# Two-stage attention with a cosine-gated feed-forward: the order of ACT's work where batch 0's h ends and batch 1's second softmax begins

## Chip, cores and metric

One core of a Trainium2 chip runs the kernel. The metric is the device time of one execution in microseconds (us); the median of three runs of the kernel before is 249.68 us (249.47 to 250.37). A difference of about 0.5% (1.25 us) is what a measurement can tell from no change.

## The reference

For each of 8 batches and 8 heads, with S = 576 positions, head dimension 64 and 32 packed queries p:

```python
p_packed = sm_attn(p, k, v)               # 32 packed rows a head
out = sm_attn(q, p_packed, p_packed)      # 576 rows a head
x = out.transpose(0, 2, 1, 3).reshape(B * S, H * D)    # 4608 x 512
h = x @ w_in                              # w_in 512 x 2048
g = h * cos(h)
return g @ w_out                          # w_out 2048 x 512, float32 out
```

`sm_attn(q, k, v)` is softmax(q kT / 8) v. All inputs are float32; the kernel loads them as bf16.

## The kernel before

The batches go through a pipeline. For batch b the steps are: `s1` (scores of p with k, exp with a running sum), `a1_pe` (transposes of these weights), `pp` (the packed values: 48 small matmuls into one psum bank, then two copies into `pp_sb`), `pp_T` (two transposes, one copy into `ppT`), `ppw` (the packed values times w_in, in four parts of 512 columns, into `PPW`), `pe_T("q", b)` (24 transposes of q in three groups of eight, each group copied out of psum into `qT`), `s2` (scores of q with the packed keys, two exps), `sums2` (row sums by a matmul with ones, then Ln), `normalise`, and then h: in 16 steps of 128 columns, two or four matmuls of `PPW` with the normalised weights, a cosine on ACT (`Sin` with a bias of pi/2) and a product on DVE that gives `gT`. Last, `out_gen` multiplies `gT` by w_out, 16 matmuls for each chunk of 128 rows. Its matmuls are the filler: `fill(n)` issues the next n of them, `set_filler` starts a new batch's, and `slot` spreads those that are left over the 16 steps of h of the next batch (`keep` of them stay for after it).

The order of each engine's work is the order in which the program issues it (a manual schedule); engines wait for one another by semaphores. Psum has eight banks. Two are output banks (pool `O`, `bank()`), taken in turn. The other six are, by `banks(3)`, three pairs `psA`, or by `banks(0)` six single banks `psH` (`one()`), taken in turn too. A tile in a bank that was used before waits for its last readers. There are three buffers for cosines, so the cosine of a step waits for the product three steps back.

The change lies in the start-up, where batch 0's h is made in single banks by `h_one` (lines 274 to 284), with batch 1 beside it (lines 437 to 470). The steps that matter, in the order issued before: the 16 steps of `h_one(0, fc)`; `pp(1)` after step 13, in an output bank; two warm matmuls (on zeros, for nothing but TensorE's activity, line 376); `pp_T(1)`; two warm matmuls; the load of ACT's table for exp (line 449); the three groups of q1's transposes, copied by ACT, DVE and DVE (line 450); four warm matmuls; issues of loads on POOL's queue; `banks(3)`; `set_filler(0)`; `s2(1)`; `ppw(1, 0)`; one filler matmul; the sums. q of batch 1 (q1) comes by a load that POOL issued much earlier (line 416).

A table load on ACT stands where the program puts it (`preload_act_table_set`). The cosines need the one set, exp and Ln the other; copies run under both.

Of the kernel before, what the change touches and what calls it, by code (L numbers as in the profile page):

```python
# [9 lines left out]
BF16 = mybir.dt.bfloat16  # L10
AF = mybir.ActivationFunctionType
ALU = mybir.AluOpType
PI_HALF = 1.5707963267948966

@with_exitstack
def kernel(
# [15 lines left out]
    NFC = DF // 128  # L32
# [14 lines left out]
    cos_pool = ctx.enter_context(tc.tile_pool(name="cos", bufs=3))  # L47
# [15 lines left out]
    V, ACT, G = nc.vector, nc.scalar, nc.gpsimd  # L63
# [19 lines left out]
    def copy(eng, out, in_):  # L83
        if eng is ACT:
            ACT.copy(out=out, in_=in_)  # L85
        else:
            eng.tensor_copy(out=out, in_=in_)  # L87

    def psa(dt=FP32):
        return psum["A"].tile([128, 2, 512 if dt == FP32 else 1024], dt, name="psA", tag="A")  # L90

    def load(n, b):
        bf[n, b] = bf_pool.tile([TP, H, C * D], BF16, name=n + "bf", tag=n + "bf", bufs=1 if n == "q" else 2)
        G.dma_start(out=bf[n, b], in_=srcs[n][b].rearrange("h (p c) d -> p h (c d)", c=C))  # L94
# [5 lines left out]
    def one(dt=FP32):  # L100
        return psum["H"].tile([128, 512 if dt == FP32 else 1024], dt, name="psH", tag="H")

    def pe_T(n, b, engs=(V, V, V), groups=(0, 1, 2), own=None):
        if 0 in groups:
            xT[n, b] = att_pool.tile([128, H * 3, TP], BF16, name=n + "T", tag=n + "T", bufs=2 if n == "k" else 1)
        t = xT[n, b]
        flat = bf[n, b].rearrange("p h x -> p (h x)")
        for i in groups:
            ps = own(BF16) if own else psa(BF16)[:, 0, :]
            for j in range(8):  # L110
                o = 8 * i + j
                nc.tensor.transpose(ps[:, j * TP:(j + 1) * TP], flat[:, o * 128:(o + 1) * 128],
                                    ident[0:TP, 0:TP])
            copy(engs[i], t[:, 8 * i:8 * i + 8].rearrange("p a x -> p (a x)"),
                 ps[:, 0:8 * TP])

    def bank(dt=FP32):
        return O.tile([128, 512 if dt == FP32 else 1024], dt, name="ot", tag="ot")
# [33 lines left out]
    def recips(b):  # L152
        r1[b] = small.tile([128, 2], FP32, name="r1")
        rs1[b] = small.tile([128, 2], FP32, name="rs1")
        V.reciprocal(r1[b], sums1[b])
        V.tensor_scalar(out=rs1[b], in0=r1[b], scalar1=scale, scalar2=None, op0=ALU.mult)
# [16 lines left out]
    def pp(b, eng=V, own=None):  # L173

        ps = own() if own else psa()[:, 0, :]
        for y in range(2):
            for j in range(C):
                c = 2 * (j % 3) + j // 3
                for x in range(4):
                    nc.tensor.matmul(ps[32 * x:32 * x + 32, y * D:(y + 1) * D],  # L180
                                     a1T[b][0:TP, y, j, 32 * x:32 * x + 32],
                                     bf["v", b][:, 2 * x + y, c * D:(c + 1) * D],
                                     start=(j == 0), stop=(j == C - 1))
        t = pp_sb[b % 2].rearrange("p a d -> p (a d)")
        copy(eng, t[:, 0:2 * D], ps[:, 0:2 * D])
        copy(eng, t[:, 2 * D:3 * D], ps[:, 0:D])

    def pp_T(b, eng=V, own=None):
        ps = own(BF16) if own else psa(BF16)[:, 0, :]
        t = pp_sb[b % 2].rearrange("p a d -> p (a d)")  # L190
        for i in range(2):
            nc.tensor.transpose(ps[:, i * 128:(i + 1) * 128], t[:, i * D:i * D + 128], ident)
        copy(eng, ppT[b % 2].rearrange("p i x n -> p (i x n)"), ps[:, 0:256])

    def ppw(b, n, eng=None, own=False, later=False, cuts=((0, 512),)):
        if b not in PPW:
            PPW[b] = ppw_pool.tile([128, 2, DF], BF16, name="PPW", tag="PPW")
        two = isinstance(eng, tuple)
        if own:
            ps = [bank(), bank()]  # L200
        else:
            t = psa()
            ps = [t[:, 0, :], t[:, 1, :]]
        for x in range(4):
            for y in range(2):
                r = slice(64 * y, 64 * y + 64)
                nc.tensor.matmul(ps[y][32 * x:32 * x + 32, :], ppT[b % 2][r, 0, x, :],  # L207
                                 w_in_bf[r, x, n * 512:(n + 1) * 512], start=True, stop=True)

        def evacuate(cuts=cuts):  # L210
            if own or two:
                for a, z in cuts:
                    for y in range(2):
                        copy(eng[y] if two else eng, PPW[b][:, y, n * 512 + a:n * 512 + z], ps[y][:, a:z])
            else:
                copy(eng or (V, ACT)[n % 2], PPW[b][:, :, n * 512:(n + 1) * 512], t)
        if later:
            return [lambda c=c: evacuate((c,)) for c in cuts]
        evacuate()
# [8 lines left out]
    def sums2(b, y):  # L228
        if b not in lns:
            lns[b] = att_pool.tile([128, 2, S], FP32, name="lns", tag="lns")  # L230
        ps = psa()
        for e in range(2):
            nc.tensor.matmul(ps[:, e, 0:HS], ones_blk, a2u[b][:, y, e * HS:(e + 1) * HS],  # L233
                             start=True, stop=True)
        ACT.activation(out=lns[b][:, y].rearrange("p (e x) -> p e x", e=2),  # L235
                       in_=ps[:, :, 0:HS], func=AF.Ln)
# [9 lines left out]
    gT, joint = {}, {}  # L246
# [22 lines left out]
    def g_tile(b):  # L269
        gT[b] = g_pool.tile([128, NFC, S], BF16, name="gT", tag="gT")  # L270
        if b % 2 == 0:
            joint[b // 2] = j_pool.tile([128, NFC, 128], BF16, name="joint", tag="joint")

    def h_one(b, fc):

        if fc == 0:
            g_tile(b)
        ps = one()
        for y in range(2):
            nc.tensor.matmul(ps, PPW[b][:, y, fc * 128:(fc + 1) * 128], a2n[b][:, y, 0:512],  # L280
                             start=(y == 0), stop=(y == 1))
        cs = cos_pool.tile([128, 512], BF16, name="cosT")
        ACT.activation(out=cs, in_=ps, func=AF.Sin, bias=PI_HALF)  # L283
        V.tensor_tensor(out=gT[b][:, fc, 0:512], in0=ps, in1=cs, op=ALU.mult)  # L284

    def h_rest(b):

# [67 lines left out]
    def fill(n):  # L355
        while n > 0 and filler[1] > 0:
            next(filler[0])
            filler[1] -= 1
            n -= 1
# [13 lines left out]
    def warm(n, wps=None, w=None):  # L373
        wps, w = bank() if wps is None else wps, wz if w is None else w
        for _ in range(n):
            nc.tensor.matmul(wps, w[:, 0:128], w, start=True, stop=True)  # L376
# [60 lines left out]
    banks(0)  # L437
    a1_pe(1, own=one)
    recips(1)
    for fc in range(NFC):  # L440
        h_one(0, fc)
        if fc in (0, 4, 8):
            ppw(0, 1 + fc // 4, (ACT, ACT if fc == 8 else V), own=True)
        if fc == 13:
            pp(1, ACT, own=bank)
    warm(2)
    pp_T(1, ACT, own=bank)
    warm(2)
    ACT.preload_act_table_set(EXP_SET)  # L449
    pe_T("q", 1, (ACT, V, V), own=one)  # L450
    warm(4)
    load("v", 2)
    load("q", 2)
    load("k", 3)
# [2 lines left out]
    set_filler(0)  # L457
    s2(1)
    ppw(1, 0, V)
    fill(1)  # L460
    sums2(1, 0)
    fill(1)
    sums2(1, 1)
# [28 lines left out]
    def cross(n, b):  # L492
# [43 lines left out]
                                in_=p_bf[:, 8:2 * B].rearrange("p g t d -> p (g t d)"))  # L536
# [73 lines left out]
```

## Time and profile before

| what | value |
|---|---|
| median of three runs | 249.68 us |
| profiled execution: time, and its span | 249.53 us, 247.6 us |
| granted TensorE clock | 1.00 |
| last h_one cosine (L283), last product (L284) start | 32.75 us, 33.73 us |
| exp table's load (L449) | 33.66 to 34.94 us |
| ACT's copy of q1's group 0 (L85) | 34.95 to 35.75 us |
| first exp of s2(1) (L225) | 36.24 us |
| first filler matmul, first sums matmul | 36.39 us, 37.03 us |

The span is the time from the first to the last recorded work; the time is 1.9 us more. Starts are in us from the span's start. PE is TensorE's matmuls, PEld its weight loads, DVE VectorE, ACT ScalarE, POOL GpSimd, SP SyncE; L283 is line 283 of the kernel before. Many copies have the line of a helper (85 on ACT, 87 on DVE), so they are told apart by their tiles: `pp_sb`, `ppT`, `qT`, `PPW`. Matmuls overlap in the rows: one of 512 columns shows 0.38 us, but the next starts 0.216 us after it.

### The profile page before, as it was taken

How to read it: one execution, taken by the hardware profiler on the slowest of the kernel's cores; microseconds unless marked ns; L12 is line 12 of the kernel's file. 1: busy time of each engine (PE TensorE's matmuls, PEld its weight loads, DVE VectorE, ACT ScalarE, POOL GpSimd, SP SyncE). 2: the span in 40 equal slices, each digit the busy share in tenths (PEclk: the TensorE clock that was granted, in tenths of full speed). 3: DMA queues.
4: the chain of work that ended last, by engine and by line, in shares of the span. 5: the costliest groups of instructions: out<-in, count | busy, mean ns of one | idle time of the engine just before them, and what ended most of it. 6: DMA issues, size and time to landing. Idle time of an engine off the chain costs nothing.

```text
span 247.6 us, 5423 instructions
## 1 busy us (share of the span) xinstructions
PE 234.0 (95%) x2204; PEld 128.3 (52%) x2240; DVE 158.5 (64%) x244; ACT 170.3 (69%) x284; POOL 38.2 (15%) x61
## 2 busy tenths in 40 slices
PE   7988889999989999999999999999999999999993
PEld 3453344566445554565446554565456554665452
DVE  3369977676549777578757666578756685774000
ACT  2369998677568777888787677978886685874110
POOL 8532330200400041005000500030000000000000
PEclk9999999999999999999999999999999999999999
DMA  6999999999899999996999894989292113111123
GB/s 88 204 209 209 202 208 228 202 235 176 135 186 173 218 146 201 189 221 122 215 214 197 148 222 109 184 172 203 63 187 59 42 45 84 43 34 53 52 75 85
DMA packets 63992, 37.37 MB, mean 151 GB/s; under 512 B 36592, under 2 KB 59376, under 8 KB 63968
## 3 DMA queue, kind: packets, MB, share of 16 engines
q0 software_dynamic: 23184, 18.81, 50.0%
q1 hardware_dynamic: 40624, 18.09, 35.6%
q8 instruction: 17, 0.28, 0.5%
q10 hardware_dynamic: 160, 0.13, 0.2%
q14 instruction: 7, 0.06, 0.1%
HBM read 37.22 MB, written 9.44 MB: 188 GB/s over the span
## 4 chain that ended last, share of the span: by engine, by line
PE 82%; DMA 6%; DVE 4%; ACT 3%; issue 2%; POOL 2%; DVEq 0%; ACTq 0%; POOLq 0%
PE ot L339 48%; PE psA L254 22%; DMA w_in_bf<-in_moe_w_in_dram 6%; PE psA L207 3%; PE psA L137 2%; PE ot L325 1%; PE psA L233 1%; PE psA L180 1%; DVE gT L284 1%; PE psH L280 1%; DVE PPW L87 1%; ACT a2u L225 1%; DVE gT L261 1%; POOL kbf L94 1%; ACT L449 1%
## 5 line engine op out<-in xcount | busy, mean ns | idle before, releaser
L339 PE MATMUL ot<-w_out_bf,gT 128*128 128x512 bf16 x482 | 128.2, 379 | 2.8 <-issue 1.9
L261 DVE TENSOR_TENSOR gT<-psA,cosT 128x576 bf16<-128x576 f32 x112 | 83.5, 757 | 32.4 <-ACT cosT L258 31.5
L258 ACT ACTIVATE cosT<-psA 128x576 bf16<-128x576 f32 x112 | 73.0, 653 | 26.4 <-PE psA L254 24.8
L254 PE MATMUL psA<-a2n,PPW 128*128 128x288 bf16 x448 | 73.2, 286 | 0.0
L339 PEld LDWEIGHTS <-gT 128*128 128x128 bf16 x512 | 47.3, 98 | 43.5 <-issue 7.8
L254 PEld LDWEIGHTS <-PPW 128*128 128x128 bf16 x448 | 43.8, 98 | 30.5 <-issue 1.0
L87 DVE CAST PPW<-psA 128x1024 bf16<-128x1024 f32 (+1 forms) x25 | 26.1, 1050 | 7.7 <-PE psA L207 6.0
L87 DVE COPY osb<-ot 128x512 f32<-128x512 f32 (+1 forms) x14 | 9.4, 671 | 21.3 <-PE ot L325 17.4
L85 ACT COPY osb<-ot 128x512 f32<-128x512 f32 (+1 forms) x23 | 13.2, 575 | 13.5 <-PE ot L339 12.4
L265 POOL COPY joint<-gT 128x512 bf16<-128x512 bf16 x14 | 8.6, 617 | 88.4 <-DVE gT L261 88.4
L243 DVE SCALAR_TENSOR_TENSOR a2n<-a2u,r,lns 128x576 bf16<-128x576 bf16 x16 | 12.4, 814 | 8.1 <-ACT lns L241 8.1
L146 ACT ACTIVATE a<-psA 128x576 bf16<-128x576 f32 x16 | 10.3, 646 | 8.3 <-PE psA L137 8.3
L235 ACT ACTIVATE lns<-psA 128x576 f32<-128x576 f32 x16 | 10.3, 651 | 6.5 <-PE psA L233 5.9
L339 PE MATMUL ot<-w_out_bf,joint 128*128 128x512 bf16 x47 | 12.6, 379 | 0.1
L376 PE MATMUL ot<-wz 128*128 128x512 bf16 (+1 forms) x23 | 10.2, 548 | 2.0 <-DVE wz L390 1.7
L225 ACT ACTIVATE a2u<-psA,rs 128x576 bf16<-128x576 f32 x16 | 11.0, 738 | 1.5 <-PE psA L137 1.4
L207 PE MATMUL psA<-w_in_bf,ppT 64*32 64x512 bf16 x224 | 10.4, 380 | 0.2
L284 DVE TENSOR_TENSOR gT<-psH,cosT 128x512 bf16<-128x512 f32 x16 | 9.9, 682 | 0.4 <-ACT cosT L283 0.4
L241 ACT ACTIVATE lns<-lns 128x576 f32<-128x576 f32 x16 | 10.0, 674 | 0.0
L85 ACT CAST PPW<-psA 128x1024 bf16<-128x1024 f32 (+1 forms) x9 | 7.4, 825 | 2.8 <-PE psA L207 2.8
L283 ACT ACTIVATE cosT<-psH 128x512 bf16<-128x512 f32 x16 | 8.7, 619 | 0.9 <-issue 0.4
L280 PE MATMUL psH<-a2n,PPW 128*128 128x512 bf16 x30 | 7.9, 381 | 0.9 <-DVE PPW L87 0.6
(90 smaller groups left out, 163.8 us busy)
## 6 DMA issues: line engine op xcount, KB each, us to landing
kbf<-in_k_dram POOLq DMA_DIRECT2D x8, 576.0 KB, 13.5
vbf<-in_v_dram POOLq DMA_DIRECT2D x8, 576.0 KB, 7.4
qbf<-in_q_dram POOLq DMA_DIRECT2D x8, 576.0 KB, 10.6
out_dram<-osb SPq DMA_DIRECT2D x24, 192.0 KB, 2.8
out_dram<-osb SPq DMA_DIRECT2D x22, 128.0 KB, 2.9
w_in_bf<-in_moe_w_in_dram POOLq DMA_DIRECT2D x4, 512.0 KB, 16.6
w_out_bf<-in_moe_w_out_dram POOLq DMA_DIRECT2D x4, 512.0 KB, 21.2
out_dram<-osb SPq DMA_DIRECT2D x26, 64.0 KB, 2.1
```

The lines of the kernel that those rows point to most:

```text
L85: ACT.copy(out=out, in_=in_)
L87: eng.tensor_copy(out=out, in_=in_)
L146: ACT.activation(out=a1[b % 2][:, y, :, 0:TP].rearrange("p (e m) x -> p e m x", e=2), in_=ps[y][:, :, 0:HS].rearrange("p e (m x) -> p e m ...
L207: nc.tensor.matmul(ps[y][32 * x:32 * x + 32, :], ppT[b % 2][r, 0, x, :], w_in_bf[r, x, n * 512:(n + 1) * 512], start=True, stop=True)
L225: ACT.activation(out=a2u[b][:, y].rearrange("p (e x) -> p e x", e=2), in_=ps[y][:, :, 0:HS], func=AF.Exp, scale=rs1[b][:, y:y + 1])
L243: V.scalar_tensor_tensor(out=a2n[b][:, y], in0=a2u[b][:, y], scalar=r1[b][:, y:y + 1], in1=lns[b][:, y], op0=ALU.mult, op1=ALU.mult)
L254: nc.tensor.matmul(ps[:, e, 0:HS], PPW[b][:, y, fc * 128:(fc + 1) * 128], a2n[b][:, y, e * HS:(e + 1) * HS], start=(y == 0), stop=(y == 1))
L258: ACT.activation(out=csv, in_=ps[:, :, 0:HS], func=AF.Sin, bias=PI_HALF)
L261: V.tensor_tensor(out=gT[b][:, fc, :].rearrange("p (e x) -> p e x", e=2), in0=ps[:, :, 0:HS], in1=csv, op=ALU.mult)
L280: nc.tensor.matmul(ps, PPW[b][:, y, fc * 128:(fc + 1) * 128], a2n[b][:, y, 0:512], start=(y == 0), stop=(y == 1))
L284: V.tensor_tensor(out=gT[b][:, fc, 0:512], in0=ps, in1=cs, op=ALU.mult)
L339: nc.tensor.matmul(pss[c], w, w_out_bf[:, fc, :], start=(fc == 0), stop=(fc == NFC - 1))
```

## The change

`h_one` is cut in three: the call issues the matmuls and gives back a function that issues the cosine, and this one gives back a function that issues the product. It also takes the bank to write to. Steps 0 to 12 are issued as before. Of the last three steps the matmuls stay in their order on TensorE, and ACT and DVE get a new order:

- ACT: the two copies of `pp(1)`, cosine 13, the copy of `pp_T(1)`, cosines 14 and 15, the copy of q1's group 0, the exp table's load. Before: cosine 13, the copies of `pp(1)`, cosines 14 and 15, the copy of `pp_T(1)`, the load, the copy of group 0.
- DVE: products 13 and 14, the copies of q1's groups 1 and 2, product 15. Before: products 13 to 15, then the copies.
- Step 15's psum is an output bank, and so the filler's first tile takes that bank.
- Two groups of two warm matmuls and one of four, in output banks, become one of four (after `pp_T`) and one of three (after q1's transposes), in psH banks.
- Ahead of the sums of batch 1 stand two filler matmuls where there was one, and `slot(1)` has one less to spread.

```diff
-    def h_one(b, fc):
+    def h_one(b, fc, own=None):
 
         if fc == 0:
             g_tile(b)
-        ps = one()
+        ps = (own or one)()
         for y in range(2):
             nc.tensor.matmul(ps, PPW[b][:, y, fc * 128:(fc + 1) * 128], a2n[b][:, y, 0:512],
                              start=(y == 0), stop=(y == 1))
-        cs = cos_pool.tile([128, 512], BF16, name="cosT")
-        ACT.activation(out=cs, in_=ps, func=AF.Sin, bias=PI_HALF)
-        V.tensor_tensor(out=gT[b][:, fc, 0:512], in0=ps, in1=cs, op=ALU.mult)
+
+        def cos():
+            cs = cos_pool.tile([128, 512], BF16, name="cosT")
+            ACT.activation(out=cs, in_=ps, func=AF.Sin, bias=PI_HALF)
+            return lambda: V.tensor_tensor(out=gT[b][:, fc, 0:512], in0=ps, in1=cs, op=ALU.mult)
+        return cos
...
-    for fc in range(NFC):
-        h_one(0, fc)
+    for fc in range(13):
+        h_one(0, fc)()()
         if fc in (0, 4, 8):
             ppw(0, 1 + fc // 4, (ACT, ACT if fc == 8 else V), own=True)
-        if fc == 13:
-            pp(1, ACT, own=bank)
-    warm(2)
+    c13 = h_one(0, 13)
+    pp(1, ACT, own=bank)
+    c13()()
+    c14 = h_one(0, 14)
+    c15 = h_one(0, 15, own=bank)
     pp_T(1, ACT, own=bank)
-    warm(2)
+    c14()()
+    rest15 = c15()
+    warm(4, one())
+    pe_T("q", 1, (ACT, V, V), (0,), own=one)
     ACT.preload_act_table_set(EXP_SET)
-    pe_T("q", 1, (ACT, V, V), own=one)
-    warm(4)
+    pe_T("q", 1, (ACT, V, V), (1, 2), own=one)
+    rest15()
+    warm(3, one())
     load("v", 2)
     load("q", 2)
     load("k", 3)
...
     ppw(1, 0, V)
-    fill(1)
+    fill(2)
     sums2(1, 0)
```

## Prediction

> **What bounds the kernel now.** First I read the page's line of engines and the busy time by stretch (columns: length, then busy us and instructions of PE, PEld, DVE, ACT, POOL, then granted clock, DMA share, GB/s).
>
> ```profile
> PE 234.0 (95%) x2204; PEld 128.3 (52%) x2240; DVE 158.5 (64%) x244; ACT 170.3 (69%) x284; POOL 38.2 (15%) x61
> ```
> ```profile
> 28.00:36.20 8.20, 7.31 (x126) 3.73 (x120) 6.94 (x12) 7.69 (x15) 2.19 (x4) 1.00 1.28 205
> 36.20:38.20 2.00, 1.39 (x21) 0.58 (x7) 1.21 (x1) 1.96 (x4) 0.50 (x1) 1.00 1.24 207
> 38.20:63.00 24.80, 24.52 (x206) 14.56 (x209) 17.54 (x26) 18.42 (x29) 2.21 (x3) 1.00 1.25 205
> ```
>
> From 38.2 us PE is the bound: 0.28 us idle of 24.80. Around the change, 28 to 38.2, it is not: there ACT is the full one (1.96 of 2.00 in the second row). So I read the chain of waits there (start, length, what).
>
> ```profile
> 32.75 0.63 ACT cosT L283
> 33.38 0.27 ACT ppT L85
> 33.64 0.02 issue
> 33.66 1.28 ACT L449
> 34.94 0.01 issue
> 34.95 0.81 ACT qT L85
> 35.76 0.04 issue
> 35.80 0.36 PE psA L137 x8
> ...
> 36.24 1.37 ACT a2u L225 x2
> 37.61 0.55 ACT lns L235
> 38.16 0.04 issue
> 38.20 0.41 PE psA L207 x8
> ```
>
> Here the exp table's load (L449) stands ahead of ACT's copy of q1, the scores (L137) wait for that copy, and the first exp (L225, 36.24) for the scores. While PE makes the scores, ACT idles 0.48 us. From the first exp the chain runs on ACT to 38.16 and goes over to PE at 38.20; after that PE hardly waits. So a microsecond gained at the first exp is one gained at the end. Third, PE's own rows, and the load of q1:
>
> ```profile
> 30.41 0.56 PE L180 MATMUL ot<-vbf,a1T 96*32 96x64 bf16 x48
> 32.44 0.27 PE L192 MATMUL ot<-ident,pp_sb 128*128 128x128 bf16 x2
> 33.16 1.20 PE L112 MATMUL psH<-ident,qbf 96*128 96x96 bf16 x24
> 36.39 0.39 PE L339 MATMUL ot<-w_out_bf,gT 128*128 128x512 bf16 x1
> 37.03 0.41 PE L233 MATMUL psA<-a2u,ones_blk 128*128 128x288 bf16 x2 [0.25 <-ACT a2u L225]
> ```
> ```profile
> L94 POOL DMA_DIRECT2D qbf<-in_q_dram x1: 801/801/801, 15.0 to 15.0; - x1
> DMA to landing us min/median/max: 18.2/18.2/18.2
> ```
>
> q1 was issued at 15.0 and landed 18.2 us later, at 33.2; its transposes begin at 33.16. So the copy of group 0 can't begin before about 33.7, whatever ACT's order is: 8 transposes at 0.043 us (24 start within 0.99 us) and the last one's 0.21 end at 33.68.
>
> **ACT, step by step.** No work goes or comes on ACT; its order changes. Starts follow each other by 0.49 us after a cosine, 0.15 and 0.10 after the two pp copies, 0.42 after the ppT copy (all starts in ACT's rows).
> - cos 12 starts at 30.92 as now. The pp product ends at 30.97, so the two pp copies go at 31.41 and 31.56 (now 32.01, 32.16), ahead of cos 13, at 31.66 (now 31.52).
> - The ppT transposes follow the second copy's end (31.79): 31.84 to 32.11. ppT is copied at 32.15 (now 33.23), cos 14 goes at 32.6 (now 32.26), cos 15 at 33.1 (now 32.75). Each cosine also needs the product three steps back on DVE (three cos buffers): those of steps 10, 11, 12 end at 31.42, 32.02, 32.62, so they don't hold them.
> - ACT is free at 33.58 and waits 0.14 for the q1 transposes. Copy of group 0: 33.72 to 34.52 (0.80). Load: 34.53 to 35.82 (1.28). First exp: 35.83, if the scores are there.
> - Gain at the first exp: 36.24 − 35.83 = 0.41 us. It is less than the 0.48 of the gap that closes plus what ACT did earlier, as q1's landing is late next.
>
> **DVE and the scores.** The scores need all three q copies, two of them on DVE. Cos 14 ends 0.33 later (33.22), so its product runs 33.25 to 33.93 (now 33.13 to 33.81). Group 1's copy waits for its transposes (34.02): 34.06 to 34.61, group 2's 34.53 to 35.08. The product of step 15, now ahead of them (33.73 to 34.41), comes after: 35.00 to 35.68. Scores: 35.12 to 35.56, under the load, with 0.26 us to spare. That the last product reads an output bank and no psH bank is what lets the scores' psA banks, cut from the psH ones, open without it.
>
> **The new wait.** The filler's first psum tile takes the output bank of step 15, so its first matmul (L339) waits for that product: 35.68. Behind it on PE stand the second filler matmul and the sums (L233), which ACT's ln and so all else need. PPW's 8 matmuls (0.41) after the scores end at about 35.8, so the wait costs nothing, and two fillers at 0.216 end at 36.2. The sums wait for the first exp's end, 35.83 + 0.74 = 36.57, anyway: 0.4 us of cover. Without it each us of lateness would cost one.
>
> **fill(1) → fill(2).** Now one filler starts at 36.39, the sums at 37.03: 0.42 idle, a second one fits. It is then one less of the 48 dealt out in slot(1) (64 − 12 − 4), where PE is the bound: −0.22. Bounds 0 (it leaves a gap there) and 0.22; I take 0.22, by the 0.28 idle us in 24.80.
>
> **The rest at nothing, and why.** Warm matmuls go from eight to seven; four start behind the ppT transposes at 31.95 and end issuing at 32.8, before q1 lands, three fill 34.19 to 34.84 before the scores. Cover gone, they would cost 0.22 each. The psH tiles they take were freed by products ended at 30.8 and 33.2. DMAs: no load changes place. On POOL the load of q2 still waits for the last q1 transpose (34.36), v2's stands ahead as now; SP's first output write is 13 us away. w_out's four parts land at 35.7, 38.9, 41.2 and 43.8 (issue plus landing); fillers 1, 9, 17 and 25 need them at 36.39, 39.85, 42.56 and 46.20 now, and at most 0.65 earlier after: the closest keeps 0.3. The later PE-bound stages only shift; from 43 us on the list of waits has PE waiting 2.7 us in total, none of it for a DMA.
>
> **Sum.** 0.41 + 0.22 = 0.63 us off the profiled execution: span 247.60 → 246.97, time 249.53 → 248.90. The runs' median is 249.68, 0.15 above that execution; from it, 249.05.
>
> **A rule against this change.** The trace first: both loads around here take 1.28 us; the first begins 0.02 after the copy ahead of it and the copy behind it begins 0.01 after. The Trainium skill, "ScalarE: Activation LUTs", section What ACT_TABLE_LOAD costs, gives the same load about 1283 ns, but adds a drain of about 1380 ns for every switch. By the page, a load placed directly ahead of the exp would delay it by that too, an estimate of 249.05 + 1.38 = 250.43. No row here has such a drain, so the sum goes without.
>
> **Rivals.**
> - **The load loses its cover (slower).** Now a late q1 hides under the load: with landing at L, the first exp comes at max(34.95, L + 0.56) + 1.28; after, at max(33.58, L + 0.56) + 2.11. At L = 33.16 the second wins by 0.41, at 33.57 they tie, from 34.39 on it loses 0.83. For it: 18.2 us in a queue at a DMA share of 1.24 to 1.3, seen once. Against: what is ahead of q1 in the queue isn't touched, and a stream that is late as a whole also delays ACT, whose work here began with w_in's landing at 19.72. Time: 249.68 + 0.83 − 0.22 = 250.29. Chance 0.12.
> - **The scores aren't hidden.** If DVE's products slip by over 0.26 (cos 14 is already 0.33 later) the exp waits for the scores again; slipping 0.66 eats the 0.41. For: DVE is full here (back to back from 30.13 to 35.34). Against: group 1's copy is held by the transposes, not by DVE. Only the filler stays: 249.46. Chance 0.13.
> - **The filler brings nothing**: its step in slot(1) becomes a gap in which cosine or product is awaited: 249.27. Chance 0.10.
> - **More than that**: one filler less moves every deal in slot(1) and the order around it; at most the 0.28 and the 1.71 idle us of PE up to 120 us (55.29 of 57.00 busy from 63) could come back. It needs most of a further 0.6 to pass 248.4. Chance 0.08.
>
> **Numbers.** The forecast has the remaining 0.57. 0.5% is about what a measurement of this kernel can tell from no change, that is 248.43 to 250.93. The forecast and both partial rivals lie within it; the late landing too, unless a run at the upper end (0.69 over the median) comes with it, a third to half of its chance. Faster 0.08, same 0.87, slower 0.05. The range, 248.5 to 250.0, holds the forecast with the runs' own scatter and the partial rivals, and leaves out the late landing and the larger gain.
>
> **What would show it.** In the profile after: pp's copies ahead of cos 13; the load starting where the group-0 copy ends, near 34.5; the exp starting at most 0.05 after the load, near 35.8; no idle time of ACT put down to L137; the step-15 product after both q copies and before the first L339; two L339 matmuls ahead of the first L233; ppw's second part near 37.8. The prediction is wrong if the exp waits for PE, if q1 lands later than 33.6, if an L339 or L233 matmul waits for L284's product, or if the 0.41 is there at 38 us and gone at 63.

## The result, and the profile after

The kernel after takes 249.09 us (median of 16 runs, 248.89 to 249.71), the kernel before, on the same chip, 249.68 us (16 runs, 249.1 to 251.22). The ratio is 0.9973, with a 95% interval of 0.9960 to 0.9985: 0.67 us, and between 0.37 and 1.0. (0.67 is also the difference of the two means, 249.81 and 249.14; the medians lie 0.59 apart.) The forecast was 249.05. But its two terms didn't both hold, as the trace shows.

The profiled execution after took 249.57 us (span 247.8), one of the longest of its kernel, so its total says nothing about the gain; its stages do. First the chain of waits from 33 to 38 us (start, length, what), which answers to the one shown of before:

```profile
33.65 0.77 ACT qT L85
34.42 0.02 issue
34.43 1.08 ACT L457
35.51 0.21 issue
35.73 0.75 ACT a2u L225
36.48 0.04 issue
36.52 0.40 PE psA L233 x2
36.92 0.22 PE ot L342
```

The copy of q1 comes first, the load (L457) behind it, and the first exp starts at 35.73 instead of 36.24. The scores (L137) are gone from the chain. (The chain books the last 0.21 us of the load as "issue"; in its row below the load runs to 35.71.) In ACT's rows of the same kernel the new order can be read, and that ACT waits for nothing any more (no bracket at the row of the exp):

```profile
31.46 0.43 ACT L85 CAST pp_sb<-ot 128x128 bf16<-128x128 f32 x2
31.71 0.69 ACT L285 ACTIVATE cosT<-psH 128x512 bf16<-128x512 f32 x1
32.25 0.41 ACT L85 COPY ppT<-ot 128x256 bf16<-128x256 bf16 x1
...
33.62 0.80 ACT L85 COPY qT<-psH 128x768 bf16<-128x768 bf16 x1
34.43 1.28 ACT L457 ACT_TABLE_LOAD   x1
35.73 1.37 ACT L225 ACTIVATE a2u<-psA,rs 128x576 bf16<-128x576 f32 x2
```

Where do the 0.51 us go? The starts of h's cosines and of the table loads, before and after, worked out from both traces:

```
                                  before    after
first exp of s2(1)                 36.24    35.73   -0.51
first cosine of slot(1)            41.40    40.89   -0.51
exp table's load after slot(1)     62.68    62.28   -0.40
pp of batch 3 (first matmul)       84.26    84.40   +0.14
last table load                   210.16   210.30   +0.14
```

Two things are lost, one after the other: 0.11 in slot(1), and 0.55 just ahead of batch 3's pp. The second one's cause stands in the waits between 78 and 96 us of the kernel after (who waited for whom: us, times, longest):

```profile
PEld L180 <- DMA a1T<-a: 1.1, 1, 1.1
PE psA L180 <- DVE PPW L87: 0.8, 1, 0.8
```

Batch 3's transposed weights, which SP sends through a DMA, landed late, at 84.36 us (before: 82.44). The row of PE's own wait names a cast on DVE. PE's rows at that place, first before, then after:

```profile
84.26 0.55 PE L180 MATMUL psA<-vbf,a1T 96*32 96x64 bf16 x48 [0.27 <-DVE gT L261]
```
```profile
84.40 0.56 PE L180 MATMUL psA<-vbf,a1T 96*32 96x64 bf16 x48 [0.82 <-DVE PPW L87]
```

In the kernel after the cast ended at 84.40, just when pp began. But pp doesn't need it: in the kernel before the same cast ran from 84.13 to 84.81, and pp began at 84.26, behind the product of L261. DVE's rows up to there are those of before, 0.41 earlier, so without the late weights pp would have begun at about 83.85. It is the weight load (PEld) that waits, for the DMA.

### The profile page after: what moved, and what is told of

Read it like the earlier page. It is cut to its first block, busy times and chain, and to the rows that moved or that the text cites. A ratio compares the mean times of both kernels' runs of the same rounds, so it can differ in the third digit from the quotient of the medians.

```text
span 247.8 us, 5456 instructions
## 1 busy us (share of the span) xinstructions
PE 238.0 (96%) x2239; PEld 128.3 (52%) x2239; DVE 158.2 (64%) x244; ACT 170.0 (69%) x284; POOL 38.1 (15%) x61
## 4 chain that ended last, share of the span: by engine, by line
PE 80%; ACT 5%; DVE 4%; issue 1%; DVEq 0%; ACTq 0%
PE ot L342 48%; PE psA L254 21%; PE psA L207 3%; PE psA L137 2%; ACT cosT L285 2%; PE psA L233 2%; DVE gT L286 1%; PE ot L328 1%; PE psA L180 1%; DVE PPW L87 1%; ACT cosT L258 1%; DVE gT L261 1%; ACT a2u L225 1%; DVE joint L300 0%; PE psA L192 0%
## 5 line engine op out<-in xcount | busy, mean ns | idle before, releaser
L342 PE MATMUL ot<-w_out_bf,gT 128*128 128x512 bf16 x512 | 133.2, 380 | 0.0
L261 DVE TENSOR_TENSOR gT<-psA,cosT 128x576 bf16<-128x576 f32 x112 | 83.5, 756 | 33.2 <-ACT cosT L258 32.2
L85 ACT COPY osb<-ot 128x512 f32<-128x512 f32 (+1 forms) x23 | 13.2, 576 | 13.5 <-PE ot L342 12.4
L243 DVE SCALAR_TENSOR_TENSOR a2n<-a2u,r,lns 128x576 bf16<-128x576 bf16 x16 | 12.4, 813 | 8.2 <-ACT lns L241 8.2
L379 PE MATMUL ot<-wz 128*128 128x512 bf16 (+1 forms) x17 | 9.0, 639 | 1.9 <-DVE wz L393 1.7
L286 DVE TENSOR_TENSOR gT<-psH,cosT 128x512 bf16<-128x512 f32 x15 | 9.3, 681 | 0.4 <-ACT cosT L285 0.4
## 6 DMA issues: line engine op xcount, KB each, us to landing
qbf<-in_q_dram POOLq DMA_DIRECT2D x8, 576.0 KB, 11.1
```

What stands on the lines that cost most here:

```text
L243: V.scalar_tensor_tensor(out=a2n[b][:, y], in0=a2u[b][:, y], scalar=r1[b][:, y:y + 1], in1=lns[b][:, y], op0=ALU.mult, op1=ALU.mult)
L261: V.tensor_tensor(out=gT[b][:, fc, :].rearrange("p (e x) -> p e x", e=2), in0=ps[:, :, 0:HS], in1=csv, op=ALU.mult)
L286: return lambda: V.tensor_tensor(out=gT[b][:, fc, 0:512], in0=ps, in1=cs, op=ALU.mult)
L342: nc.tensor.matmul(pss[c], w, w_out_bf[:, fc, :], start=(fc == 0), stop=(fc == NFC - 1))
```

## The experiments

All were run beside the kernel before on the same chip; a ratio is against that kernel. One number serves throughout: how long after the first matmul of batch 1's pp the first exp of `s2(1)` starts. Both stand behind the same earlier work, so it is free of what happened before 30 us, as long as q1's landing doesn't set the exp. It is 5.83 in the kernel before and 5.28 in the execution after shown above, where q1's landing did set it.

**1. The load back ahead of the copy.**

```diff
-    pe_T("q", 1, (ACT, V, V), (0,), own=one)
     ACT.preload_act_table_set(EXP_SET)
+    pe_T("q", 1, (ACT, V, V), (0,), own=one)
     pe_T("q", 1, (ACT, V, V), (1, 2), own=one)
```

> The kernel after, with the exp table's load put back ahead of ACT's copy of q1's group 0; all else as after. Theory (the gain is made where the load hides the scores): ACT is free at 33.55, loads to 34.85, copies to 35.65, the scores follow and the first exp starts near 36.13, 0.40 later than after: about 249.5. Rival 1 (the gain comes from the earlier pp copies, the output bank and the fuller fillers): the exp may move, the time stays near 249.1. Rival 2 (the gain is only a narrower scatter of the landings): 249.1 to 249.7, with the exp's start following q1's landing.

Measured: 249.45 us, ratio 1.0004 [0.9990, 1.0019], no gain left. ACT's rows:

```profile
33.44 1.28 ACT L456 ACT_TABLE_LOAD   x1
34.73 0.80 ACT L85 COPY qT<-psH 128x768 bf16<-128x768 bf16 x1
36.02 1.37 ACT L225 ACTIVATE a2u<-psA,rs 128x576 bf16<-128x576 f32 x2 [0.48 <-PE psA L137]
```

The 0.48 us of idle ahead of the exp is back, and the exp starts 5.79 after pp (before: 5.83). With everything else of the change in place, the earlier pp copies and the output bank are worth 0.04 here. The gain hangs on the order of copy and load; rival 1 falls. Nor is rival 2, a narrower scatter of the landings alone, enough: q1 landed at 33.01 us here and at 33.02 in the kernel after, and the exp came at 36.02 and not at 35.73.

**2. One filler matmul instead of two.**

```diff
     ppw(1, 0, V)
-    fill(2)
+    fill(1)
     sums2(1, 0)
```

> The kernel after, with one filler matmul instead of two ahead of the sums. Theory after reading the trace (the second filler is given back in slot(1), whose cosines and copies set its pace): first exp unchanged near 35.7, slot(1) ends within 0.1 of where it ended after, time 249.0 to 249.15. Rival (the prediction's term): 0.22 slower, 249.3.

Measured: 249.31 us, ratio 0.9981 [0.9962, 1.0000]. The runs lie up to 1.8 us apart (248.70 to 250.52), so the time doesn't decide. The trace does: from the first cosine of slot(1) to the next table load 21.27 us pass, as before (21.28); in the kernel after 21.39. This held in every trace of the study: 21.27 to 21.28 in the seven with one filler ahead of the sums, 21.39 to 21.40 in the seven with two. The second filler is not worth 0.22 us, it costs 0.11. PE's rows from 53 us show one place, first before, then after:

```profile
54.03 0.65 PE L254 MATMUL psA<-a2n,PPW 128*128 128x288 bf16 x4
54.63 0.50 PE L112 MATMUL psA<-ident,kbf 96*128 96x96 bf16 x8
54.97 0.81 PE L339 MATMUL ot<-w_out_bf,gT 128*128 128x512 bf16 x3
```
```profile
53.52 0.65 PE L254 MATMUL psA<-a2n,PPW 128*128 128x288 bf16 x4
54.33 0.50 PE L112 MATMUL psA<-ident,kbf 96*128 96x96 bf16 x8 [0.16 <-ACT kT L85]
54.67 0.81 PE L342 MATMUL ot<-w_out_bf,gT 128*128 128x512 bf16 x3
```

Four matmuls of 288 columns take 0.49 us, so 0.11 us of idle stand behind them before, and 0.32 after: with the deal moved, k2's transposes come before ACT has emptied the bank they need. At 49.3 us it is the same: one filler fewer is dealt ahead of step 6's matmuls (two and not three by the program; of the three of before, only two have a record in the trace), and 0.30 us of idle, waiting for a product on DVE, stand there instead of 0.09. A third gap, 0.11, is gone; in sum the 0.22 saved and 0.11 more are spent waiting.

This trace shows a second thing. PE's waits from 16 to 18.5 us:

```profile
PE ot L112 <- DMA kbf<-in_k_dram: 0.9, 1, 0.9
```

k1's load, unchanged and issued at 5.0 us in all kernels, landed 12.4 us later here and 11.4 later in the trace before; and as k1's transposes stand between the sums of batch 0, pp of batch 1 came at 30.96 instead of 30.41. Of the twelve traces of the study in which k1's load is unmoved, eight have it 11.1 to 11.6 us after its issue, four (experiments 2, 3, 4 and 8) 12.4 to 12.7. With a late k1 pp thus came 0.55 us later and more, which is one cause that the scatter of the runs can have; runs without a trace can't be sorted by it. The first exp stands 5.20 after pp here.

**3. The swap alone, in the kernel before.**

```diff
-    ACT.preload_act_table_set(EXP_SET)
-    pe_T("q", 1, (ACT, V, V), own=one)
+    pe_T("q", 1, (ACT, V, V), (0,), own=one)
+    ACT.preload_act_table_set(EXP_SET)
+    pe_T("q", 1, (ACT, V, V), (1, 2), own=one)
```

> The kernel before, with nothing but ACT's copy of q1's group 0 put ahead of the exp table's load. Theory: ACT copies from 33.7 to 34.5 and loads to 35.82; DVE, in its old order, ends the last q copy at 35.34, so the scores run 35.39 to 35.83 and the exp starts near 35.9: 0.33 to 0.36 earlier than before, about 249.3. Rival (the other parts are needed: the output bank and the product's place keep the scores from being late): the exp stays within 0.15 of 36.24, no difference from before.

Measured: 249.33 us, ratio 0.9987 [0.9969, 1.0006]. In the trace k1 was late (pp at 31.24), and the exp stands 5.42 after pp, 0.41 nearer than before: two lines of the change make 0.41 of the 0.63 that the whole change gives where k1 is late (5.20, experiment 2). Most of what is left is DVE, which in the old order makes product 15 ahead of the q copies (they end at 36.17 here); ACT's exp waits for the scores again (start, length, the bracket is idle time):

```profile
35.20 1.28 ACT L450 ACT_TABLE_LOAD   x1
36.67 1.37 ACT L225 ACTIVATE a2u<-psA,rs 128x576 bf16<-128x576 f32 x2 [0.18 <-PE psA L137]
```

**4. Two fillers alone, in the kernel before** (`fill(1)` to `fill(2)`).

> The kernel before, with nothing but two filler matmuls instead of one ahead of batch 1's sums. Theory (given back in slot(1)): first exp as before, time within 0.1 of before. Rival (the prediction's term): 0.22 faster. A third way: the second filler delays the sums, by 0.0 to 0.1, as there are 0.42 us of idle for its 0.22.

Measured: 250.36 us, ratio 1.0021 [1.0003, 1.0040]. No gain: the runs are, if anything, longer. The exp stands 5.83 after pp, so the sums aren't delayed, and slot(1) takes 21.39. The rival's 0.22 is off by its sign, and the theory's nothing by 0.1.

**5 and 6. q1 landing 2.5 us later**, in the kernel before and after:

```diff
-    load("q", 1)
-    for n in range(4):
+    load_w_out(0)
+    load("q", 1)
+    for n in range(1, 4):
         load_w_out(n)
```

> The kernel before, with the load of q1 issued behind the first part of w_out instead of ahead of it, so that q1 lands about 2.5 us later (near 35.7). Theory (the load hides a late q1): with L the start of q1's transposes, ACT has loaded the table by 34.95 and waits; copy at L + 0.56, first exp at L + 1.84, near 37.5, about 1.3 us later than before: 250.6. A late k1 hardly shows, as L sets the time. Rival (ACT's own order of work sets it): the exp stays within 0.5 of 36.24.

> The kernel after, with the same later load of q1. Theory (the copy ahead of the load takes the load's cover away): copy at L + 0.56, load, first exp at L + 2.67, near 38.4: 0.83 later than in the kernel before with the same late load, 0.9 to 1.0 longer with the second filler's cost: about 251.5. Rival (the change is better whatever q1 does): it keeps 0.3 or more of its lead over the kernel before with the late load.

Measured: 252.99 us, ratio 1.0136 [1.0108, 1.0164], and 252.56 us, ratio 1.0107 [1.0078, 1.0135]. The kernel after was not the longer one, against the theory, and the first exps came at 39.64 and 38.76 instead of 37.5 and 38.4. But the pair can't decide: while PE waited for q1 its clock fell. The busy times by stretch of the first of them (the number behind POOL's is the granted clock):

```profile
33.00:35.60 2.60, 0.22 (x2) 0.03 (x2) 1.47 (x3) 1.98 (x3) 0.00 (x0) 1.00 1.27 204
35.60:39.00 3.40, 3.40 (x28) 2.30 (x28) 1.12 (x2) 0.80 (x1) 1.04 (x2) 0.51 1.25 207
```

2.4 us without a matmul were followed by 3.4 us at half clock, in which the transposes and the four warm matmuls went at half speed, ahead of the scores. In the second, 2.7 us without a matmul were followed by 3.4 us at half clock from 36.43 on, over the three warm matmuls and the scores.

**7 and 8. q1 landing 1.25 us later, with the clock kept up.** The load stands between two halves of w_out's first part, and five more warm matmuls stand ahead of q1's transposes:

```diff
-    load("q", 1)
-    for n in range(4):
+    load_w_out(0, 0, 2)
+    load("q", 1)
+    load_w_out(0, 2, 4)
+    for n in range(1, 4):
         load_w_out(n)
```

> The kernel before, with q1's load issued between two halves of w_out's first part (so that it lands about 1.25 us later, near 34.4) and five more warm matmuls ahead of q1's transposes, which keep TensorE from idling while it waits. Theory (the table's load hides it): first exp at max(34.95, L + 0.56) + 1.28, 36.24 to 36.3 with L near 34.4, as before without the delay; with the same TensorE clock all along, 249.3 to 249.5 when k1 lands early. Rival (any delay of q1 shows): 1.25 later.

> The kernel after, with the same later load and five more warm matmuls. Theory (the copy waits, and the table's load waits behind it): first exp at L + 2.67, near 37.05, 0.8 later than in the kernel before with the same delay, and with the second filler's 0.11 about 0.9 longer. Rival (the change keeps its lead): first exp before 36.2.

Measured: 250.07 us, ratio 1.0012 [0.9996, 1.0028], and 250.64 us, ratio 1.0045 [1.0027, 1.0063]. Now the kernel after is the longer one, by 0.57. With L the start of q1's transposes (34.19 and 34.74; in the second, k1 was late and the nine warm matmuls end only at L), the first exp came at L + 2.43 before and at L + 2.66 after. ACT's rows of the second:

```profile
35.29 0.80 ACT L85 COPY qT<-psH 128x768 bf16<-128x768 bf16 x1 [0.89 <-PE psH L112]
36.10 1.28 ACT L459 ACT_TABLE_LOAD   x1
37.40 1.37 ACT L225 ACTIVATE a2u<-psA,rs 128x576 bf16<-128x576 f32 x2
```

The sum for the kernel after was right (L + 2.67). For the kernel before it wasn't: 36.61 and not 36.3. Its chain says why:

```profile
34.19 1.19 PE psH L112 x24
35.38 0.86 PE ot L376 x4
36.24 0.30 PE psA L137 x8
36.54 0.03 ACTq L225
36.57 0.04 issue
36.61 1.37 ACT a2u L225 x2
```

Behind a late q1 the load is hidden, as claimed, but all 24 transposes, DVE's two copies (they ended at 36.10) and the scores are not. (The chain goes by the four warm matmuls between them on PE instead. The last one began at 35.87, so the scores could follow at 36.08: without the copies too they would have come only 0.1 earlier than at 36.17.) So the price of the lost cover is 2.66 − 2.43 = 0.23 us, and not 0.83. With the second filler's 0.11 that makes 0.34 of the 0.57 in the times; the rest isn't settled (L itself differs by 0.56 in these two executions).

**9 and 10. k1 made late in every execution**, by issuing it between two halves of w_in's first part, before and after:

```diff
-    load("k", 1)
-    for n in range(3):
+    load_w_in(0, 0, 2)
+    load("k", 1)
+    load_w_in(0, 2, 4)
+    for n in range(1, 3):
         load_w_in(n)
```

> The kernel before, with w_in's first part loaded in two halves and k1's load issued between them, so that k1 lands late (near 17.6) in every execution and the rest of the stream stands as it was. Theory (the executions fall in two groups by whether k1 lands near 16.4 or 17.5): the runs form one group, the late one, near 250.3 with pp of batch 1 at 31.1 and the first exp 5.83 after it. Rival (the groups come from something else): two groups again, 249.3 and 250.3.

> The kernel after, with k1 late in the same way. Theory (with everything up to h later, q1 has landed in good time, and ACT's order alone sets the copy, so the earlier pp copies count too): first exp 5.20 after pp of batch 1, 0.63 earlier than in the kernel before with a late k1; less 0.11 for the second filler, 0.5 shorter, near 249.7. Rival (the gain is the same 0.3 in both groups): first exp 5.4 after pp, 0.3 shorter.

Measured: 252.95 us, ratio 1.0134 [1.0101, 1.0166], and 251.90 us, ratio 1.0090 [1.0065, 1.0114]. k1 came later than meant (its transposes at 18.74 and 19.34, with 3.4 us at half clock from 20.4 and 20.5), and the expected times were missed by 2.2 to 2.7 us. The runs of the kernel before with a late k1 still form two groups (252.1 to 252.2 and 253.7 to 254.2), as the rival had it: whether k1's landing still varied or the groups come from something else, one trace of each kernel can't tell. What the pair does settle is the number: 5.83 from pp to the exp before, 5.20 after, 0.63 us. When pp comes late enough for q1 to lie ready, the gain is 0.63 and not 0.41.

**11. After, unchanged, once more.**

> The kernel after, unchanged, beside the others on the same chip. Theory: two groups of executions by k1's landing, 0.3 below those of the kernel before where k1 is early and 0.5 where it is late; first exp 5.20 after pp of batch 1 where q1 has landed in time; slot(1) takes 22.09 again. The 0.56 that the first execution lost at pp of batch 3 comes back only if the transposed weights land after 83.5. Rival (that loss belongs to the change): it is there again.

Measured: 249.17 us, ratio 0.9988 [0.9972, 1.0003]. Exp 5.20 after pp, slot(1) 21.39, and no loss at batch 3's pp: the stages from there on run 0.23 ahead of the trace before, in which pp of batch 1 stood 0.29 earlier: together 0.52. The theory's part on k1 was wrong here: k1 landed 11.3 us after its issue, yet pp came at 30.70, since the first transposes, k0's, came 0.65 later than before (8.27 for 7.62). The interval is wide: it holds no difference as well as the first measurement's 0.9973.

The rows of the late DMA, in this execution (first) and in that of the kernel after that lost 0.55 us:

```profile
L160 SPq DMA_TRANSPOSE a1T<-a x1: 4830/4830/4830, 70.6 to 70.6; - x1
...
DMA to landing us min/median/max: 12.2/12.2/12.2
```
```profile
L160 SPq DMA_TRANSPOSE a1T<-a x1: 4630/4630/4630, 70.5 to 70.5; - x1
...
DMA to landing us min/median/max: 13.9/13.9/13.9
```

Issued at the same time, they landed at 82.8 and 84.4; pp began at 84.03 here and would have begun at about 83.85 there. Landing shortly before them (by 0.2 to 0.5 us, and by 0.2 to 0.8 in all fourteen traces) is the load of k4, the last of three that POOL issues from 66.3 us on in this execution and from 67.75 in the one that lost, when k3's transposed copy has landed. That copy was late in turn behind q2's load, which was issued at 34.6 in both and landed at 55.36 here and at 56.24 there; SP transposes q2 before k3. Both links, from q2's load to k4's and from there to the weights, are argued from these times; neither was tried. So it isn't the change alone. In the kernel before, with pp at 84.26, weights landing at 84.36 would have cost about 0.14; the change uses up the rest of the slack, as PE gets there 0.41 earlier and the landing doesn't.

**12. A version that should beat both**: after with one filler, and q1's groups of 6, 9 and 9.

```diff
+    def pe_T(n, b, engs=(V, V, V), groups=(0, 1, 2), own=None, at=(0, 8, 16, 24)):
...
-    pe_T("q", 1, (ACT, V, V), (0,), own=one)
+    pe_T("q", 1, (ACT, V, V), (0,), own=one, at=(0, 6, 15, 24))
     ACT.preload_act_table_set(EXP_SET)
-    pe_T("q", 1, (ACT, V, V), (1, 2), own=one)
+    pe_T("q", 1, (ACT, V, V), (1, 2), own=one, at=(0, 6, 15, 24))
...
-    fill(2)
+    fill(1)
```

> The kernel after with one filler matmul ahead of the sums, as before the change, and q1's transposes in groups of 6, 9 and 9 instead of 8, 8 and 8. Theory: ACT's copy is 0.18 shorter and can start 0.09 sooner, DVE's two end at 35.1, so the scores and the load end together and the first exp comes 0.15 to 0.2 earlier against pp of batch 1 than in the kernel with one filler (5.0 instead of 5.20), or near 35.55 when q1's landing sets it; slot(1) takes 21.98 and not 22.09. Together 0.25 to 0.3 shorter than the kernel after. Rival (the scores, behind DVE's longer copies, now end last): the exp no earlier than after, 0.1 shorter, by the filler alone.

Measured: 249.62 us, ratio 0.9991 [0.9974, 1.0007]; the lowest five runs are 248.69 to 249.10, the rest up to 250.40. The stage went as expected in part: the exp starts 2.55 after q1's transposes begin (after: 2.66), at 35.77 and not 35.55, with the scores behind DVE's longer copies as the last to come, as the rival had it; and slot(1) takes 21.28 (the expected texts count it from a point 0.70 us earlier), so that 0.47 us were in hand up to 81 us. Then batch 3's weights landed at 84.4 again (PE's waits, 78 to 96 us):

```profile
PE psA L180 <- DMA a1T<-a: 1.0, 1, 1.0
```

This took 0.70 back, and the same wait at batch 4's pp 0.25 more. The version is not shown to beat the kernel after; what it gained early in this execution, late weights took.

## Why the prediction came out right, and where it was wrong

- **The copy ahead of the load: right, and the gain hangs on it.** Forecast 0.41, with the exp at 35.83; measured 0.51 and 35.73, of which 0.09 is q1's transposes starting earlier in that execution (33.07 for 33.16). Against their start the forecast was 2.67 and the trace says 2.66. Experiment 1 takes the gain away (0.04 is left), and experiment 3, the swap alone, makes 0.41 of the 0.63 of a late k1.
- **What is late next: right for an early pp.** ACT is free about 0.1 us before q1's transposes of group 0 are through. Where pp comes 0.3 us later or more, q1 is there, and the change's other parts (pp copies, product 15 behind the q copies) bring it to 0.63 (experiments 2, 10 and 11). The prediction worked from one execution and didn't see that the start of this stage moves.
- **The filler: the failed step.** "It is then one less of the 48 dealt out in slot(1) (64 − 12 − 4), where PE is the bound: −0.22", by the 0.28 us of idle in 24.80. Measured +0.11 in seven traces against seven. A full PE doesn't say that a step taken out comes back: the deal moves, and 0.33 us of waits for ACT and DVE appear where a filler had covered them. The rival that gave it nothing was nearer, and still too kind.
- **The new wait: right.** The first filler started at 35.71, product 15 ended at 35.58, the sums came at 36.52 behind the first exp. The scores had 0.14 us to spare (35.57 against the load's end at 35.71), not 0.26.
- **"none of it for a DMA": wrong where it mattered.** The list of waits of before shows waits, not what would be one with PE 0.4 us earlier. The prediction's own sign looked as far as 63 us, where 0.40 of the gain was still there; at 84 it was gone. Three traces were ahead of before by 0.2 us or more at 80 us: after (0.41), experiment 12 (0.47) and experiment 11 (0.23). The first two lost 0.55 and 0.70 to batch 3's weights.
- **The load's lost cover: the mechanism is there, its price was 0.83 and is 0.23** (experiments 7 and 8; at experiment 7's L of 34.19 the forecast's two terms lie 0.63 apart). The term left out DVE's copies and the scores behind a late q1: L + 2.43 in the kernel before, and not 36.23.
- **No drain.** The load ended at 35.71 and the exp started at 35.73. The Trainium skill's 1380 ns ("ScalarE: Activation LUTs", What ACT_TABLE_LOAD costs) don't show in any of the traces, in either order; the load's 1.28 us do.

So the sum that the traces support is 0.42 (the 0.51 less the 0.09 of an earlier q1) to 0.63 at the first exp, less 0.11: 0.31 to 0.52, and less again where the weights land late. The total of 0.63 was near the measured 0.67 (0.37 to 1.0) partly by luck, as one of its two terms has the wrong sign. The larger gain where pp is late makes up for some of that. Another part may be how many long runs fell to each side: of the 16 runs before, five took over 250 us, of the 16 after none. Over the runs below 250 us alone the means differ by 0.39, and by 0.34 in experiment 11 (nine of 32 and two of 12 left out), which is what the traces support. But this bound was drawn with the runs in view, and the change may itself have a share in the long ones. How often k1 or the weights come late in runs that aren't profiled isn't known, and so how the 0.67 comes out of these parts stays open.

## What to carry to other kernels

When an engine must switch its table, put the switch where the engine would wait anyway: behind the work that lets others start, beside what they do, and count what stands behind a late input on both orders. A PE that is full doesn't mean that a step less of filler is time won; look at what the step was covering. And a gain in front can be lost at the next transfer whose landing doesn't move with it, so list the landings and their slack, not only the waits.

## What the runs showed of the hardware

- The same load, issued at the same time in the same queue, landed 11.1 to 12.7 us later (k1), and batch 3's transposing DMA 10.8 to 14.0 us after its issue. With a late k1 pp of batch 1 came 0.55 to 0.83 us later than in the trace before (experiments 2, 3, 4 and 8); late weights moved pp of batch 3 by 0.55 and 0.70.
- 1.9 to 2.7 us without a matmul were followed by 3.4 us at half clock (1.92 and 2.47 us in experiments 9 and 10, 2.38 and 2.71 in 5 and 6). The Trainium skill, "TensorE: Matmul & The Clock Gate", section What's actually happening, names a free-running window of about 3.4 us, an idle one of which brings the half clock; the slow stretch had that length, the idle time ahead of it was shorter in all four.
